# Attention followed by a PReLU MLP: the result parts turned by VectorE in 32x32 blocks and placed by the store, instead of by TensorE and ScalarE

## The chip, the cores and the metric

The kernel runs on one core of a Trainium2 chip. The metric is the device time of one execution in microseconds (us), as the median of several executions. A core has five engines that run side by side and wait for one another by semaphores: PE (TensorE, the matrix unit; its weight loads are shown apart as PEld), DVE (VectorE), ACT (ScalarE), POOL (GpSimd) and SP (SyncE, which here only issues DMA transfers). SBUF is the working memory, with 128 partitions; PSUM is the small memory that PE writes its products to, in eight banks.

## What is computed

The reference, cut to what matters:

```python
# q, k, v: (4, 8, 768, 64); proj: (64, 6)
q_bucket = np.sum((np.einsum('bhsd,dk->bhsk', q, proj) > 0) * 2 ** np.arange(6), axis=-1)
k_bucket = np.sum((np.einsum('bhsd,dk->bhsk', k, proj) > 0) * 2 ** np.arange(6), axis=-1)
mask = q_bucket[:, :, :, None] == k_bucket[:, :, None, :]
scores = np.where(mask, scale * np.matmul(q, k.transpose(0, 1, 3, 2)), -1e9)
attn = np.exp(scores - np.max(scores, axis=-1, keepdims=True))
attn = attn / (np.sum(attn, axis=-1, keepdims=True) + 1e-09)
x = np.matmul(attn, v)                 # then (B,H,S,D) -> (B*S, H*D): 3072 x 512
# w_in: (512, 2048), w_out: (2048, 512), alpha: (2048,)
h = x @ w_in
g = np.maximum(h, 0.0) + alpha * np.minimum(h, 0.0)
out = g @ w_out                        # 3072 x 512, float32
```

An attention in which a query sees only the keys of its own hash bucket, and then two matrix products with a PReLU between them.

## The kernel before

The attention runs first, in 32 units `u` (16 pairs of heads, two halves of the queries each). While it runs, DVE and ACT also prepare the weights of the MLP. Then come 60 blocks of products, for each of the 4 batches 8 blocks `ff1` (names `f` in the profile) and 7 blocks `ff2` (names `z`). The products use a scheme with seven multiplications instead of eight at two levels (a Strassen form), so that each block needs sums of its operands, which DVE makes, and a block of `ff2` has seven steps of eight matmul instructions.

The result of `ff2` is kept transposed: `m2[b, p]` holds output columns in its partitions (`i` is the upper or lower 128 of 256) and tokens in its free dimension. `turn_out` brings it into the order of the output. It runs when a part is complete, four times for each batch, 16 times in all.

```python
    def load_w2(b, n):
        if n < 7:
            t = late[0].tile([P, NI, 2 * H2], F32, name=f"wl{b}_{n}", tag="wl")
            nc.sync.dma_start(t, w_out_s[SIDES[ORDER[n]][0]])
            for m, kh, dh in ((0, 0, 0), (1, 1, 0), (2, 1, 1), (21, 0, 1)):
                w2[b, n, m] = t[:, kh * HK : (kh + 1) * HK, dh * H2 : (dh + 1) * H2]
    # ... cut ...
    def turn_out():
        while to_turn:
            b, p, half, ch = to_turn.pop(0)
            ps = two_banks(f"to{b}_{p}")
            flat = ps.rearrange("p a f -> p (a f)")
            for t in range(CH):                                   # CH = 3
                for i in range(2):
                    do(PE.transpose(flat[:, 2 * t * P + i * P :][:, :P], m2[b, p][:, i, t * P : (t + 1) * P], ident))
            o = late[0].tile([P, CH, 2 * P], F32, name=f"o{b}_{p}", tag="o")
            do(ACT.copy(o.rearrange("p t d -> p (t d)"), flat[:, : CH * 2 * P]))
            nc.sync.dma_start(
                out_v[b, ch * CH : (ch + 1) * CH].rearrange("c p d -> p c d")[:, :, half * 2 * P : (half + 1) * 2 * P], o,
            )
```

`do` keeps the compute instructions of each engine in the order of the program. The tile pools decide by themselves when a buffer is free, and the transfers may be moved. The block loop (cut):

```python
    for j, (b, what, n) in enumerate(blocks):
        # ... step 2 and its finish, sums for the next block ...
        if j:
            now.step(5); now.step(6); now.step(3)
            turn_out()
            sum_w2(b, n2, 6)
            now.step(7)
            sum_w2(b, n2, 5); sum_g2(b, n2, 5)
        # ... loads of later weights; in the last ff2 block of a batch the four sum_x ...
        before = now
        if j + 1 < len(blocks):
            now = ...                       # the next product
            now.step(1)
        before.step(4)
        # ...
    turn_out()
```

The parts of the attention that the change touches:

```python
    def setup():
        # ...
        ps = psum.tile([P, 512], F32, name="nil", tag="av")
        for i in range(12):                                       # matmuls on zeros while the first loads are under way
            do(PE.matmul(ps, zero[:, :P], zero, start=True, stop=True))

    def setup_alpha():
        ps = psum.tile([P, NF], F32, name="alps", tag="sm")
        # ...
    # in the loop over the units:
        attend(u, 0)          # probabilities times values, key blocks 0, 1, 2 -> tile av
        totals(u)             # ones times the summed probabilities accd -> tile sm
        # ... weight work of DVE ...
        attend(u, 1)          # key blocks 3, 4, 5
        divide(u)
```

Of the kernel before, what the change touches and what calls it, by code (L numbers as in the profile page):

```python
# [8 lines left out]
F32 = mybir.dt.float32  # L9
# [338 lines left out]
@with_exitstack  # L348
def kernel(
    ctx: ExitStack,  # L350
    tc: tile.TileContext,
    q: bass.AP,
    k: bass.AP,
    v: bass.AP,
    proj: bass.AP,
    moe_w_in: bass.AP,
    moe_w_out: bass.AP,
    moe_alpha: bass.AP,
    out: bass.AP,
):  # L360

    args = (tc, q, k, v, proj, moe_w_in, moe_w_out, moe_alpha, out)
    keep = ctx.enter_context(tc.tile_pool(name="keep", bufs=1))
    flag = keep.tile([1, 1], mybir.dt.int32, name="flag")
    fast_path(*args, flag)
    again = tc.nc.values_load(flag[0:1, 0:1])
    with tc.If(again > 0):  # L400
        general_path(*args)
# [3 lines left out]
def fast_path(  # L405
# [12 lines left out]
    nc = tc.nc  # L418
# [78 lines left out]
    def setup():  # L497

        zero = const.tile([P, 512], BF16, name="zero")
        do(DVE.memset(zero, 0.0))  # L500
        do(DVE.memset(wh, 0.0))
        for s in range(2):
            nc.sync.dma_start(wh[D * s : D * s + D, :NB], proj)
        nc.sync.dma_start(alpha16, moe_alpha.rearrange("(t p) -> t p", p=P))
        make_identity(nc, ident)
        do(DVE.memset(ones, 1.0))

        ps = psum.tile([P, 512], F32, name="nil", tag="av")
        for i in range(12):
            do(PE.matmul(ps, zero[:, :P], zero, start=True, stop=True))  # L510

        do(DVE.memset(hb, 0.0))
        for r in range(0, P, 32):
            do(DVE.memset(hb[r : r + 2 * NB], 1.0 if r % D else -1.0))
            do(DVE.memset(hb[r : r + NB], -1e-37))
        for t in pts:
            do(POOL.memset(t[:, :, CW : CW + 1], 1.0))
        for t in qbs:
            do(POOL.memset(t, 0.0))

    def setup_alpha():
        ps = psum.tile([P, NF], F32, name="alps", tag="sm")
        do(PE.transpose(ps, alpha16, ident[:NF, :NF]))
        do(DVE.tensor_copy(alpha, ps))

# [111 lines left out]

    BOTH = slice(0, 2)

    def turn(pi, name, halves=BOTH):  # L640

        src = nat[name, pi].rearrange("p c h d -> p c (h d)")
        if halves.start == 0:
            tr[name, pi] = pool.tile([P, S], F32, name=f"{name}T{pi}", tag=f"{name}T")
        ps = two_banks(f"tp_{name}{pi}")
        for c in range(CH * halves.start, CH * halves.stop):
            do(PE.transpose(ps[:, c // CH, c % CH * P :][:, :P], src[:, c], ident))
        do(ACT.activation(
            tr[name, pi].rearrange("p (h w) -> p h w", h=2)[:, halves], ps[:, halves, :CW], AF.Copy,
            scale=DOWN if name == "q" else 1.0,  # L650
        ))

    def magnitude(pi, name):

# [66 lines left out]
        do(DVE.tensor_tensor(accd[u], accd[u], accp[u], op=ALU.add))  # L721


    def attend(u, half):
        pi, g = divmod(u, NCH)
        if half == 0:
            av[u] = psum.tile([P, 512], F32, name=f"av{u}", tag="av")
        w = CW + 1 if g == 0 else CW
        for kc in range(half * NC // 2, (half + 1) * NC // 2):
            for s in range(2):  # L730
                do(PE.matmul(  # L731
                    av[u][D * s : D * s + D, :w], nat["v", pi][:, s, kc * D : (kc + 1) * D], prob[u, kc][:, s, :w],
                    start=(kc == 0), stop=(kc == NC - 1),
                ))
        if half == 1 and g == 0:
            vsum[pi] = pool.tile([P, 1], F32, name=f"vs{pi}", tag="vs")
            do(DVE.tensor_scalar(vsum[pi], av[u][:, CW : CW + 1], EPS, None, op0=ALU.mult))

# [135 lines left out]
    def load_w2(b, n):  # L874

        if n < 7:
            t = late[0].tile([P, NI, 2 * H2], F32, name=f"wl{b}_{n}", tag="wl")
            nc.sync.dma_start(t, w_out_s[SIDES[ORDER[n]][0]])
            for m, kh, dh in ((0, 0, 0), (1, 1, 0), (2, 1, 1), (21, 0, 1)):
                w2[b, n, m] = t[:, kh * HK : (kh + 1) * HK, dh * H2 : (dh + 1) * H2]  # L880

    def sides_g(b, n):
        t = g_m[b, SIDES[ORDER[n]][1]]
# [54 lines left out]
    def turn_out():  # L938
        while to_turn:
            b, p, half, ch = to_turn.pop(0)  # L940
            ps = two_banks(f"to{b}_{p}")
            flat = ps.rearrange("p a f -> p (a f)")
            for t in range(CH):
                for i in range(2):
                    do(PE.transpose(flat[:, 2 * t * P + i * P :][:, :P], m2[b, p][:, i, t * P : (t + 1) * P], ident))
            o = late[0].tile([P, CH, 2 * P], F32, name=f"o{b}_{p}", tag="o")
            do(ACT.copy(o.rearrange("p t d -> p (t d)"), flat[:, : CH * 2 * P]))
            nc.sync.dma_start(
                out_v[b, ch * CH : (ch + 1) * CH].rearrange("c p d -> p c d")[:, :, half * 2 * P : (half + 1) * 2 * P], o,
            )  # L950


    top = const.tile([P, 4], F32, name="top")
# [29 lines left out]
    setup()  # L983
    load_part(0, "q", slice(CH, NC), nc.sync)
    load_part(0, "k", slice(CH, NC), nc.scalar)
    for name in "qk":
        turn(0, name, first)
    hash_bits(0, first)
    for name in "qk":
        turn(0, name, second)  # L990
    load(1, "q")
    load(1, "k")
    load_weight(0)
# [16 lines left out]
    for u in range(UNITS):  # L1010
        pi, g = divmod(u, NCH)
        scores(u, 1)
        if u < last:
            scores(u + 1, 0)
        add_last(u)
        add_total(u)
        if u < last:
            add_first(u + 1)
        else:
            now = ff1(0, 0)  # L1020
            now.step(1)
            now.step(5)
        if g == 0 and pi + 1 < NPAIR:
            hash_bits(pi + 1)
        if g == 1 and pi + 2 < NPAIR:
            turn(pi + 2, "q")
            turn(pi + 2, "k")
        if u < last:
            weight_parts(u + 1)
        else:  # L1030
            weight_sums(4)
        attend(u, 0)
        totals(u)
        if u < last:
            weight_sum(u + 1)
            weight_sums(1 if u < HW - 1 else 2)
            weight_group(u + 1)
        attend(u, 1)
        divide(u)
        if g == 1 and pi + 2 < NPAIR:  # L1040
            load(pi + 2, "v")
        load_weight(u + 4)
        if u == HW + 2:
            load_w(0)
            load_w(1)
            load_x(0)
        if HW + 4 <= u < HW + 8:
            sum_x(0, u - HW - 4, DVE)
        if u + 2 < NW:
            weight_abs(u + 2)  # L1050
        if u == 1:
            setup_alpha()
        if g == 1:
            for name in "qk":
                magnitude(pi, name)
                if pi + 3 < NPAIR:
                    load(pi + 3, name)
# [8 lines left out]
    for j, (b, what, n) in enumerate(blocks):  # L1066
        n2 = n + 1 if what == "2" else 0 if n == NI - 1 else 7
        if n2 == 0:
            sides_g(b, 0)
            sum_w2(b, 0, 3, 4)  # L1070
        now.step(2) if j else now.step(6)
        if j == 0:
            now.step(3)
            now.step(7)
            now.step(2)
        now.step(22)
        if j == 4:
            largest()
        if 0 < n2 < 7:
            sides_g(b, n2)  # L1080
            sum_w2(b, n2, 3, 4)
        if n2 < 7:
            sum_g2(b, n2, 3, 4)
        if j:
            now.step(5)
            now.step(6)
            now.step(3)
            turn_out()
            sum_w2(b, n2, 6)
            now.step(7)  # L1090
            sum_w2(b, n2, 5)
            sum_g2(b, n2, 5)
        if j == 4:
            verdict()
        if what == "1":
            load_w(b * NI + n + 2)
            if n >= NI - 2:
                load_w2(b, n - NI + 2)
        else:
            load_w2(b, n + 2)  # L1100
            if b + 1 < B:
                if n == 0:
                    load_x(b + 1)
                if n == 6:
                    for m in range(4):
                        sum_x(b + 1, m, DVE)
        before = now
        if j + 1 < len(blocks):
            b1, what1, n1 = blocks[j + 1]
            now = ff1(b1, n1) if what1 == "1" else ff2(b1, n1)  # L1110
            now.step(1)
        before.step(4)
        if n2 < 7:
            sum_g2(b, n2, 6)
    turn_out()
# [1 line left out]
_INS = ['q', 'k', 'v', 'proj', 'moe_w_in', 'moe_w_out', 'moe_alpha']  # L1117
_OUTS = [((3072, 512), 'float32')]
# [25 lines left out]
```

## Time and profile before

| | before |
|---|---|
| time, median of 3 | 924.33 us (924.19 to 925.03) |
| span of the profiled execution | 923.9 us |
| PE busy | 907.8 us (98%) |
| DVE busy | 754.0 us (82%) |
| ACT busy | 422.6 us (46%) |
| attention | from the start to about 363 us |
| one batch of the MLP | about 139 us: 73 us of `f` blocks and 66 us of `z` blocks |

The page of the profile gives the busy time of each engine and, for groups of like instructions, their number, their mean duration and the idle time ahead of them, with what ended that idle time. A line such as "L945 PE MATMUL to<-ident,m 128*128 128x128 f32 x96" is one group: source line 945, engine PE, a matrix instruction that writes tile `to` from `ident` and `m`, and there were 96 of them. For a matmul the first name after the arrow is the operand that streams through, the second the one that is loaded as weights. In a timeline, "[2.87 <-DMA wl]" after a row says that the engine stood idle for 2.87 us until a transfer to `wl` landed. PE's instructions overlap, so the distance from start to start of consecutive ones is their cost, not their duration.

### The profile page before, as it was taken

To read this page: it belongs to the slowest core of one execution; us is meant where nothing else is said; L and a number is where in the kernel's file an instruction comes from. 1 tells how busy PE (TensorE), PEld (TensorE's weight loads), DVE (VectorE), ACT (ScalarE), POOL (GpSimd) and SP (SyncE) were. 2 spreads that over 40 slices of the span, in tenths; PEclk is the share of its full clock that TensorE was granted. 3 is DMA by queue.
4 is the path that set the end of the run, shared out by engine and by line. 5 is a ranking of instruction groups with operands and counts; after the bars stand their busy time and mean duration, and the time that the engine had idled before them with its cause. 6 is when DMAs were issued, how large, how long until landed. Compare 5 with 4: busy or idle time off the path is not lost.

```text
span 923.9 us, 13627 instructions
## 1 busy us (share of the span) xinstructions
PE 907.8 (98%) x5073; PEld 605.4 (66%) x5073; DVE 754.0 (82%) x1316; ACT 422.6 (46%) x751; POOL 40.9 (4%) x50
## 2 busy tenths in 40 slices
PE   7999999999999999999999999999999999999996
PEld 4444444454444444556998556998556998556996
DVE  3899998999999998678987668978668978668985
ACT  7788888888877783222212222212222212222212
POOL 1111111111111110000000000000000000000000
PEclk9999999999999999999999999999999999999999
DMA  9576969798777844425333325334325333321232
GB/s 240 145 188 158 273 162 301 177 254 240 189 188 190 205 131 148 174 92 186 110 134 131 116 101 180 109 131 140 112 105 177 111 133 138 112 105 40 100 131 70
DMA packets 114059, 141.50 MB, mean 153 GB/s; under 512 B 54064, under 2 KB 102208, under 8 KB 110400
## 3 DMA queue, kind: packets, MB, share of 16 engines
q1 hardware_dynamic: 103680, 127.56, 43.4%
q0 software_dynamic: 8704, 12.58, 8.0%
q8 instruction: 42, 0.69, 0.3%
q10 hardware_dynamic: 1600, 0.39, 0.2%
q14 instruction: 33, 0.27, 0.1%
HBM read 100.67 MB, written 27.26 MB: 138 GB/s over the span
## 4 chain that ended last, share of the span: by engine, by line
PE 65%; DVE 16%; DMA 2%; issue 1%; ACT 0%; DVEq 0%; ACTq 0%
PE sc L698 3%; PE z_4a L805 2%; PE f_4a L805 2%; PE z_7a L805 2%; PE z_5a L805 2%; PE z_3a L805 2%; PE z_6a L805 2%; PE z_2a L805 2%; PE z_1a L805 2%; PE f_2a L805 2%; PE f_5a L805 2%; PE f_7a L805 2%; PE f_6a L805 2%; PE f_1a L805 2%; PE av L731 2%; PE f_0a L805 2%
## 5 line engine op out<-in xcount | busy, mean ns | idle before, releaser
L703 ACT ACTIVATE pt<-sc 128x768 f32<-128x768 f32 x192 | 153.1, 814 | 61.8 <-PE sc L698 60.1
L698 PE MATMUL sc<-qT,kT 64*128 64x384 f32 x768 | 155.1, 482 | 0.0
L731 PE MATMUL av<-pt,vn 128*64 128x385 f32 (+1 forms) x768 | 136.5, 491 | 0.0
L731 PEld LDWEIGHTS av<-pt,vn 128*64 128x64 f32 x768 | 52.3, 136 | 70.7 <-issue 63.8
L698 PEld LDWEIGHTS sc<-qT,kT 64*128 64x128 f32 x768 | 68.1, 188 | 34.8 <-issue 34.7
L855 DVE TENSOR_TENSOR g<-g,g 128x384 f32<-128x384 f32 x128 | 68.4, 555 | 2.2
L698 PE MATMUL sc<-qb,kb 64*128 64x384 bf16 x384 | 63.0, 324 | 2.8 <-ACT kb L684 2.2
L895 DVE TENSOR_TENSOR ws<-wl 128x512 f32<-128x512 f32 x56 | 38.5, 688 | 24.0 <-DMA wl<-w_out_s 24.0
L903 DVE TENSOR_TENSOR gs<-g,gs 128x768 f32<-128x768 f32 x56 | 53.5, 956 | 1.0
L903 DVE TENSOR_TENSOR gs<-g 128x768 f32<-128x768 f32 x56 | 53.4, 953 | 0.0
L713 POOL DMA_DIRECT2D accp<-pt x32 | 38.5, 1204 | 311.4 <-DVE accp L712 150.2
L851 DVE SCALAR_TENSOR_TENSOR g<-h,alpha 128x384 f32<-128x384 f32 x32 | 19.8, 618 | 36.0 <-ACT h L844 36.0
L698 PEld LDWEIGHTS <-kb 64*128 64x128 bf16 x384 | 19.2, 94 | 43.2 <-issue 19.9
L712 DVE TENSOR_TENSOR accp<-pt,pt 128x768 f32<-128x768 f32 x32 | 30.4, 951 | 10.0 <-ACT pt L703 10.0
L679 ACT ACTIVATE qb<-hs,hb 32x384 bf16<-32x384 f32 x64 | 36.7, 574 | 2.2 <-issue 1.1
L721 DVE TENSOR_TENSOR accd<-accd,accp 128x768 f32<-128x768 f32 x32 | 30.7, 958 | 5.1 <-DMA accp<-pt 4.1
L717 DVE TENSOR_TENSOR accd<-pt,pt 128x768 f32<-128x768 f32 x32 | 30.5, 952 | 3.6 <-ACT pt L703 3.6
L718 DVE TENSOR_TENSOR accd<-accd,pt 128x768 f32<-128x768 f32 x32 | 30.7, 959 | 3.3
L915 DVE TENSOR_TENSOR m<-m,m 128x768 f32<-128x768 f32 (+1 forms) x40 | 28.6, 716 | 1.9 <-ACT m L921 1.2
L743 PE MATMUL sm<-accd,ones 128*64 128x384 f32 x128 | 26.5, 492 | 3.2 <-DVE accd L721 3.1
L684 ACT ACTIVATE kb<-hs,hb 64x384 bf16<-64x384 f32 (+1 forms) x48 | 27.7, 578 | 0.6
L564 DVE TENSOR_SCALAR_CACHE_REDUCE wx<-wx 128x512 f32<-128x512 f32 x32 | 21.7, 679 | 2.9 <-ACT wx L558 2.9
(323 smaller groups left out, 1777.7 us busy)
## 6 DMA issues: line engine op xcount, KB each, us to landing
wi<-w_in_s SPq DMA_DIRECT2D x32, 896.0 KB, 4.6
wl<-w_out_s SPq DMA_DIRECT2D x28, 1024.0 KB, 4.8
accp<-pt POOLq DMA_DIRECT2D x32, 384.0 KB, 4.3
raw<-in_moe_w_in_dram SPq DMA_DIRECT2D x16, 512.0 KB, 4.0
raw<-in_moe_w_out_dram SPq DMA_DIRECT2D x16, 512.0 KB, 3.8
w_in_s<-wsi SPq DMA_DIRECT2D x16, 448.0 KB, 5.4
w_out_s<-wso SPq DMA_DIRECT2D x8, 896.0 KB, 5.5
vn<-in_v_dram SPq DMA_DIRECT2D x16, 384.0 KB, 4.5
```

The lines of the kernel that those rows point to most:

```text
L679: do(ACT.activation(bits["q", pi][D * s : D * s + 32, cols], ps[c : c + 32, half, :CW], AF.Sign, bias=hb[c : c + 32],))
L698: do(PE.matmul(sc[:, s, :CW], what["k", pi][r, ks], what["q", pi][r, qs], start=first, stop=not first,))
L703: do(ACT.activation(pt[:, :, :CW], sc[:, :, :CW], AF.Exp, scale=SCALE / DOWN))
L713: nc.gpsimd.dma_start(accp[u], p(u, 2), accum_op=ALU.add)
L717: do(DVE.tensor_tensor(accd[u], p(u, 3), p(u, 4), op=ALU.add))
L718: do(DVE.tensor_tensor(accd[u], accd[u], p(u, 5), op=ALU.add))
L721: do(DVE.tensor_tensor(accd[u], accd[u], accp[u], op=ALU.add))
L731: do(PE.matmul(av[u][D * s : D * s + D, :w], nat["v", pi][:, s, kc * D : (kc + 1) * D], prob[u, kc][:, s, :w], start=(kc == 0), stop=(kc = ...
L805: do(PE.matmul(self.ps[bank], self.left(left, k), self.right(right, k), start=start and k == 0, stop=k == self.nk - 1, skip_group_check=no ...
L855: do(DVE.tensor_tensor(new_g(b, to)[:, i], g_m[b, x][:, i], g_m[b, y][:, i], op=ALU.subtract))
L895: do(DVE.tensor_tensor(t, w2[b, n, x], w2[b, n, y], op=op))
L903: do(DVE.tensor_tensor(t, g2[b, n, x], g2[b, n, y], op=ALU.subtract))
```

## The change

The main part: an `m2` part is no longer turned by PE (six 128x128 transposes into PSUM) and moved by ACT (a copy of 128x768). DVE turns it in 32x32 blocks, with two instructions of 128x384, one for each `i`, straight from SBUF to SBUF. A turn in 32x32 blocks puts each block right inside, but leaves the blocks of the four partition groups where they are. The store then puts the blocks in place: twelve transfers of 32 partitions x 4 x 64 elements, instead of one of 128 x 3 x 256. So that a row piece in memory is 64 elements long (256 bytes) and not 32, the two halves `i` are not the upper and lower 128 columns any more but the even and odd ones: DVE writes half `i` to every second element of `o`, and the weights of `ff2` are read as every second column of the loaded tile. `turn_out` moves to the end of the block, behind the sums. The very last part is still turned by PE and ACT, in two pieces with a store each.

Small parts: at the start 8 instead of 12 matmuls on zeros, and DVE instead of ACT copies the turned `k` of pair 0; `alpha` is turned in another PSUM buffer; and in each unit of the attention `totals` comes after five of the six key blocks instead of three.

The diff, cut to its core:

```diff
-        for i in range(12):
+        for i in range(8):
             do(PE.matmul(ps, zero[:, :P], zero, start=True, stop=True))
 ...
-        ps = psum.tile([P, NF], F32, name="alps", tag="sm")
+        ps = two_banks("alps")[:, 0, :NF]
 ...
+        if engine is DVE:
+            do(DVE.tensor_copy(dst, ps[:, halves, :CW]))
+        else:
+            do(ACT.activation(dst, ps[:, halves, :CW], AF.Copy, scale=DOWN if name == "q" else 1.0))
 ...
-                w2[b, n, m] = t[:, kh * HK : (kh + 1) * HK, dh * H2 : (dh + 1) * H2]
+                w2[b, n, m] = t.rearrange("p n (f i) -> p n i f", i=2)[:, kh * HK : (kh + 1) * HK, dh]
 ...
     def turn_out():
         while to_turn:
             b, p, half, ch = to_turn.pop(0)
-            ps = two_banks(f"to{b}_{p}")
-            ... six PE.transpose, o, ACT.copy, one dma_start ...
+            o = late[0].tile([P, CW, 2], F32, name=f"o{b}_{p}", tag="o")
+            for i in range(2):
+                do(DVE.transpose(o[:, :, i], m2[b, p][:, i]))
+            src = o.rearrange("p (c w d) i -> p c w (d i)", c=CH, d=32)
+            for a in range(DM // 128):
+                for c in range(CH):
+                    cols = slice(half * DM // 2 + 64 * a, half * DM // 2 + 64 * a + 64)
+                    nc.sync.dma_start(
+                        out_v[b, ch * CH + c].rearrange("(w r) d -> r w d", r=32)[:, :, cols],
+                        src[32 * a : 32 * a + 32, c],
+                    )
+
+    def turn_last():
+        ((b, p, half, ch),) = to_turn
+        ps = two_banks("to").rearrange("p a f -> p (a f)").rearrange("p (t i f) -> p t i f", i=2, f=P)
+        o = late[0].tile([P, CH, P, 2], F32, name="o_last", tag="o")
+        for ts in ((2,), (0, 1)):
+            for i in range(2):
+                for t in ts:
+                    do(PE.transpose(ps[:, t, i], m2[b, p][:, i, t * P : (t + 1) * P], ident))
+            ts = slice(ts[0], ts[-1] + 1)
+            do(ACT.copy(o[:, ts].rearrange("p t f i -> p t i f"), ps[:, ts]))
+            ... one dma_start of o[:, ts] ...
 ...
-    for name in "qk":
-        turn(0, name, first)
-    hash_bits(0, first)
-    for name in "qk":
-        turn(0, name, second)
+    for half in (first, second):
+        turn(0, "q", half)
+        turn(0, "k", half, DVE)
+        if half is first:
+            hash_bits(0, first)
 ...
-        attend(u, 0)
+        attend(u, range(NC - 1))
         totals(u)
 ...
-        attend(u, 1)
+        attend(u, range(NC - 1, NC))
         divide(u)
 ...
             now.step(3)
-            turn_out()
             sum_w2(b, n2, 6)
 ...
+        turn_out()
         before = now
 ...
-    turn_out()
+    turn_last()
```

More of the change, by code (lines that the diff above doesn't have):

```diff
@@ L638, in fast_path, with turn @@
     BOTH = slice(0, 2)
-    def turn(pi, name, halves=BOTH):
+    def turn(pi, name, halves=BOTH, engine=None):
         src = nat[name, pi].rearrange("p c h d -> p c (h d)")
@@ L647, in turn @@
             do(PE.transpose(ps[:, c // CH, c % CH * P :][:, :P], src[:, c], ident))
[L648 to L651, printed above, removed]
+        dst = tr[name, pi].rearrange("p (h w) -> p h w", h=2)[:, halves]
+        if engine is DVE:
+            do(DVE.tensor_copy(dst, ps[:, halves, :CW]))
+        else:
+            do(ACT.activation(dst, ps[:, halves, :CW], AF.Copy, scale=DOWN if name == "q" else 1.0))
     def magnitude(pi, name):
@@ L721, in add_total, with attend @@
         do(DVE.tensor_tensor(accd[u], accd[u], accp[u], op=ALU.add))
-    def attend(u, half):
+    def attend(u, kcs):
         pi, g = divmod(u, NCH)
-        if half == 0:
+        if kcs.start == 0:
             av[u] = psum.tile([P, 512], F32, name=f"av{u}", tag="av")
         w = CW + 1 if g == 0 else CW
-        for kc in range(half * NC // 2, (half + 1) * NC // 2):
+        for kc in kcs:
             for s in range(2):
@@ L734, in attend @@
                 ))
-        if half == 1 and g == 0:
+        if kcs.stop == NC and g == 0:
             vsum[pi] = pool.tile([P, 1], F32, name=f"vs{pi}", tag="vs")
@@ L940, in turn_out @@
             b, p, half, ch = to_turn.pop(0)
-            ps = two_banks(f"to{b}_{p}")
[L942 to L950, printed above, removed]
+            o = late[0].tile([P, CW, 2], F32, name=f"o{b}_{p}", tag="o")
[19 more added lines that the diff above has]
+            do(ACT.copy(o[:, ts].rearrange("p t f i -> p t i f"), ps[:, ts]))
+            dst = out_v[b, ch * CH : (ch + 1) * CH].rearrange("c p d -> p c d")
+            nc.sync.dma_start(dst[:, ts, half * 2 * P : (half + 1) * 2 * P], o[:, ts].rearrange("p t f i -> p t (f i)"))
     top = const.tile([P, 4], F32, name="top")
```

## The prediction

> **What bounds the kernel now.** I began with the page: engines, slices, chain.
>
> ```profile
> PE 907.8 (98%) x5073; PEld 605.4 (66%) x5073; DVE 754.0 (82%) x1316; ACT 422.6 (46%) x751; POOL 40.9 (4%) x50
> ...
> DVE  3899998999999998678987668978668978668985
> ...
> PE 65%; DVE 16%; DMA 2%; issue 1%; ACT 0%; DVEq 0%; ACTq 0%
> ```
>
> PE is busy for 98% of the span and carries most of the chain that ended last, so what leaves PE shortens the run, unless another engine then makes PE wait. DVE comes next: it holds 16% of the chain, and the chain listed by stretches has it from about 154 to 277 us, in the attention. In the MLP (from the 16th slice on) the chain lies on PE. Busy time by stretches, for the `z` and `f` blocks of the first batch (columns: length, PE, PEld, DVE, ACT, POOL, clock, DMA share, GB/s):
>
> ```profile
> 432.24:497.94 65.70, 65.70 (x408) 65.04 (x406) 57.32 (x91) 13.90 (x38) 0.00 (x0) 1.00 0.39 135
> 497.94:571.20 73.26, 73.12 (x235) 43.63 (x235) 50.27 (x89) 19.64 (x41) 0.00 (x0) 1.00 0.36 123
> ```
>
> PE never rests in the `z` stage, and DVE is at 57.32 / 65.70 = 87%. The timeline around one `turn_out` (start, length):
>
> ```profile
> 456.97 1.46 PE L805 MATMUL z_5c<-g,ws 128*128 128x192 f32 x8
> ...
> 458.27 0.82 PE L945 MATMUL to<-ident,m 128*128 128x128 f32 x6
> ...
> 458.92 1.47 PE L805 MATMUL z_5a<-gs,ws 128*128 128x192 f32 x8
> 459.12 0.80 ACT L947 COPY o<-to 128x768 f32<-128x768 f32 x1 [1.58 <-PE to L945]
> 459.95 0.39 SPq L948 DMA_DIRECT2D out_dram<-o  x1
> ```
>
> A step of eight matmuls takes 458.27 - 456.97 = 1.30 us, 162.5 ns each, and the six transposes push the next step back by 458.92 - 458.27 = 0.65 us, 108 ns each. ACT's copy stands on nobody's path. Last, what PE waited for over the run:
>
> ```profile
> PE sm L743 <- DVE accd L721: 3.1, 6, 0.8
> PE sc L698 <- ACT kb L684: 2.2, 2, 1.2
> PE nil L510 <- DVE wh L501: 1.2, 1, 1.2
> PE alps L523 <- DVE st L753: 1.0, 1, 1.0
> PE to L945 <- DVE m L915: 0.7, 1, 0.7
> ```
>
> These few microseconds are what the small parts can win.
>
> **What the Trainium skill says.** "VectorE: DVE Perf Modes", The three transpose paths: DVE turns 32x32 blocks only, so the transfers have to place them. The trace agrees on what such an instruction costs: the attention's own turns of 128x384 took 574 and 578 ns. "SBUF — State Buffer", Door 1 (its note on cachelines): SBUF is read in lines of 16 bytes and a stride is free while at least two elements fall into each line, thus every second fp32. No instruction of the trace before reads weights that way, so the run has to show it. "TensorE: Matmul & The Clock Gate", LDWEIGHTS: a load takes the number of columns / 1.2, 107 ns for 128. The trace agrees: a transpose with its own weight load passes every 108 ns. "DMA: Bandwidth & Descriptors", Specifications: transfers under 512 B per piece are not at line rate. The trace agrees loosely: the `q` loads in 256-byte pieces land in 4.3 us (192 KB, 768 pieces), the stores of `x` of the same size in longer rows in 3.5 us.
>
> **The change, part by part.**
>
> *Removed from PE and ACT.* Of 16 parts, 15 leave PE: 15 x 0.65 = 9.75 us. The fifteenth lies in the last block, where it belongs to the tail, so 14 x 0.65 = 9.1 us come out of the stream of full steps. ACT loses 15 x 0.80 us, off the path.
>
> *Added to DVE.* 30 instructions; by the attention's turns 0.58 us each, 1.15 us for a part. Two parts fall into a batch's `z` stage, the third about its end, the fourth into the first `f` block. The `z` stage goes to 57.3 + 2.3 = 59.6 us of DVE in 65.7 - 1.95 = 63.75: 93%. Is it in time? DVE's timeline has idle stretches of 0.25, 1.48, 2.87, 0.88 and 0.25 us in the second to sixth `z` block, all while `wl` is landing. Part 2 comes in the third block (1.48 idle, of which 0.65 go because the block gets shorter), part 3 in the sixth (0.25). Part 3 leaves DVE about 1.5 us late. In that block the sum `gs_4_3` is ready at 488.28 and its step begins at 492.25: 4.0 us of slack. The tightest buffer, the PSUM bank `c`, is read by DVE until 489.5 and written again at 492.25. So no wait of PE comes from this.
>
> *Strided weights.* Steps 1, 2 and 4 of seven read `wl` directly: 672 of the 1568 `z` matmuls. A load needs at most 108 ns (the transposes) and has 162.5 ns: it could grow by half before it shows. I count 0.
>
> *The stores.* 12 transfers instead of one. An issue takes 0.32 us for the 128-piece stores of `x` and 0.39 us for the stores of `o`; 12 x 0.33 = 4.0 us of SP for each part. By the order of the built program the loads of `wl` and `wi` keep their places: part 2's stores come behind `wl_4`, part 3's behind `wl_0` of the next batch, part 4's behind the first free `wi`. The next load comes a block (9.1 us) later, and SP is free again. In 1536 pieces of 256 B a store takes more time in the DMA engines than before, but their share is 0.39 and 0.36 here. I count 0 until the tail.
>
> *The tail.* In the last block PE saves the 0.65 us of part 5. I replay the end with the times of before: step 7 at 912.22 instead of 912.87, step 4 at 914.15, the last sums of DVE till 916.47, and the two turns of part 5 just before (914.9 to 916.0). The last piece is turned by four transposes and a copy of 2/3 of the size, ready at about 917.6 instead of 918.77. But SP issues in order, and part 5's twelve stores stand first: 916.05 + 4.0 = 920.0, then the two last ones; the last issue is at about 920.4, where it was at 918.80. The tail gets 1.6 us longer. MLP in sum: -9.1 + 1.6 = -7.5.
>
> *The start.* The matmuls on zeros begin at 1.19 us; their weight loads stand about 0.42 us apart up to the eighth, at about 4.1, and the last four fit into 0.75 us. Turning begins at 5.18 us. With eight it could begin at about 4.35, when the first `q` (issue at 0.74 to 1.7, 2.4 to 2.5 us to landing) is there. The chain on ACT and PE up to the first exponential then moves by 0.8 us: -0.8. DVE's copy of `k` shortens only what is already parallel for the first half, and frees 0.49 us of ACT before the first exponential, which waits for PE: 0.
>
> *`totals` later.* Four more matmul pairs (8 x 0.162 = 1.3 us) stand ahead of it. The waits are 0.8 us at most in the row above; by starts, `av` to `sm` is 1.99 us undisturbed (45.62 to 47.61) and 2.91 at the worst (347.09 to 350.00), so 0.92. Each is covered. Where DVE is the limit the gain is one time 1.3 us for each stretch in which PE has caught up with it: 0.7 at the first unit, 1.3 at 261 to 300, 1.0 in the last two units: -3.0. `divide` still has the next unit's scores (4.95 us) to finish under.
>
> *`alpha`.* PE's wait of 1.0 us goes, but a score buffer is held until DVE has its copy: -0.3.
>
> Sum: 924.3 - 7.5 - 0.8 - 3.0 - 0.3 = 912.7; I take 913.
>
> **Rivals.** *The strided weight loads become the limit.* For it: PEld is busy for 65.04 of 65.70 us in the `z` stage, and such a read is untried here. Against it: these 190 ns loads overlap, and the transposes pass in 108 ns. If a strided load took double (216 ns), 672 x 53 ns = 36 us would come on top: about 949. *DVE becomes the bound of the `z` stage.* For it: 93%, and turns that write every second element, or sums that read so, may be slower than the 0.58 and 0.69 us used. If each turn took 1.0 us, two parts would ask for 1.7 us more of each `z` stage's 4.1 spare; only with the 13 sums on `wl` also slower would PE wait, by some microseconds for each batch: 915 to 925. *The stores delay the loads.* The part 2 stores are in the engines with `wl_4`; `wl` landed at 468.05 and step 1 of its block began at 469.16, so 1.1 us late is enough. For it: 1536 small pieces. Against it: the load is issued first. If every store cost a wait of 1 us: 15 us, and nothing is gained. *The tail hides.* If the issue of a small store is faster (0.2 us), the tail costs nothing: 911.
>
> **Range and chances.** The core is well founded: 9.1 us of PE time counted from starts. The small parts (-4.1) could come to half or to a little more, the tail to between 0 and 3, late loads or DVE to several. Eight in ten: 908 to 920. Faster by over 2% would need under 905.8 and has no source in this sum: 0.03. Slower by over 2% (over 942.8) is only the strided weights: 0.06. Within 2%: 0.91.
>
> **What would show it.** Right: the steps beside a turn stand 1.30 us apart without a gap; steps on `wl` take 1.30 us like those on `ws`; DVE turns of about 0.58 us; no PE wait for `wl`, `wi` or `ws` in the MLP; twelve issues in about 4 us, the last store behind them. Wrong: `wl` steps over 1.30 us, PE waits for DVE `gs` or `ws` in the `z` blocks, a wait for a DMA, or a first turn that still begins at about 5 us.

## The result, and the profile after

| | before | after |
|---|---|---|
| time, median | 924.26 us (923.65 to 925.1) | 921.38 us (920.55 to 923.39) |
| ratio to before, 95% interval | 1 | 0.997 (0.9957 to 0.9983) |
| span of the profiled execution | 923.9 us | 920.6 us |

The change brings 2.9 us, where 11 were predicted. The page of the changed kernel, engines and chain:

```profile
PE 896.8 (97%) x4979; PEld 596.7 (65%) x4979; DVE 768.4 (83%) x1348; ACT 409.5 (44%) x735; POOL 40.9 (4%) x50
...
PE 76%; DVE 16%; DMA 4%; issue 1%; SPq 1%; ACT 1%; DVEq 0%; ACTq 0%; POOLq 0%
```

PE lost 11.0 us of work and DVE took over 14.4, as meant. But the span fell by less than a third of what PE lost, and the chain that ended last now has SyncE's queue in it (SPq 1%), which it had not before. Busy time by stretches, again for the `z` and the `f` blocks of the first batch:

```profile
431.88:495.62 63.74, 63.74 (x390) 63.15 (x389) 58.38 (x94) 11.47 (x35) 0.00 (x0) 1.00 0.42 135
495.62:567.87 72.25, 72.25 (x230) 43.11 (x230) 52.77 (x95) 18.80 (x40) 0.00 (x0) 1.00 0.41 129
```

The `z` stage is 63.74 us long (65.70 before) and PE never rests in it; DVE is at 58.38, or 92%. The timeline around a turn (start, length):

```profile
461.82 1.46 PE L808 MATMUL z_6b<-g,wl 128*128 128x192 f32 x8
...
463.12 1.46 PE L808 MATMUL z_6c<-gs,ws 128*128 128x192 f32 x8
...
464.42 1.46 PE L808 MATMUL z_6a<-gs,ws 128*128 128x192 f32 x8
...
464.78 1.03 DVE L946 STREAM_TRANSPOSE o<-m 128x384 f32<-128x384 f32 x2
465.72 1.46 PE L808 MATMUL z_6c<-g,ws 128*128 128x192 f32 x8
...
465.84 4.14 SPq L952 DMA_DIRECT2D out_dram<-o  x9
```

The steps stand 1.30 us apart, past the turn and no matter whether the weights are summed ones (`ws`) or every second column of the loaded tile (`wl`). Nine small stores take SP 4.14 us. So the middle of the kernel does what was wanted. The end does not. SP's queue in the last 21 us (start, length of a row of issues), first before, then after, with two narrower cuts:

```profile
918.80 0.37 SPq L948 DMA_DIRECT2D out_dram<-o  x1
```

```profile
900.60 12.65 SPq L952 DMA_DIRECT2D out_dram<-o  x24
913.35 1.74 SPq L969 DMA_DIRECT2D out_dram<-o_last  x2
...
906.55 6.70 SPq L952 DMA_DIRECT2D out_dram<-o  x12
...
914.70 0.40 SPq L969 DMA_DIRECT2D out_dram<-o_last  x1
```

Part 3's twelve stores are just out when part 5's twelve begin at 906.55, and the two of the last part, whose first piece ACT copied at 907.54, stand behind them till 914.70. PE is done at about 908.6. What PE waited for:

```profile
PE av L734 <- DVE x L762: 2.3, 4, 0.9
PE sc L701 <- ACT kb L687: 2.2, 2, 1.1
PE sc L701 <- DVE alpha L526: 1.7, 1, 1.7
PE to L965 <- ACT o_last L967: 1.3, 1, 1.3
PE nil L512 <- DVE wh L503: 1.2, 1, 1.2
PE f_2a L808 <- DMA wi<-w_in_s: 1.1, 2, 0.7
```

The 3.1 us for `sm` and the 1.0 for `alps` are gone from the top. In their place stand a wait of the values product `av` for DVE's division (2.3), one of the attention products `sc` for `alpha`'s copy (1.7), and one of the third `f` product for its input weights (1.1).

**The theory, and its rival.** To compare runs I cut each profiled span at three starts of PE: of the step `f_1b` in the first batch, of the first `f_2a`, and of the last `z_4b`. The table has the length of each stretch in us; the kernels below the second row are the experiments told in the next section.

| kernel | to `f_1b` | to `f_2a` | to the last `z_4b` | to the end | span |
|---|---|---|---|---|---|
| before | 371.17 | 6.45 | 529.40 | 16.8 | 923.9 |
| after | 369.85 | 7.31 | 520.55 | 22.9 | 920.6 |
| main part only | 370.61 | 6.45 | 520.01 | 23.7 | 920.7 |
| small parts only | 369.88 | 6.87 | 529.25 | 16.8 | 922.8 |
| late parts 3 and 5 on PE | 368.75 | 6.74 | 520.52 | 17.2 | 913.3 |
| stores on two queues | 368.68 | 7.05 | 520.64 | 20.4 | 916.7 |
| `alpha` back | 369.15 | 6.80 | 519.96 | 23.4 | 919.3 |
| totals back | 370.45 | 6.45 | 519.91 | 23.4 | 920.2 |
| input weights first | 371.78 | 6.45 | 519.94 | 23.8 | 922.0 |
| late part 5 on PE | 369.43 | 6.80 | 520.28 | 17.0 | 913.6 |
| the best: late part 5 on PE, own buffer, input weights first | 370.42 | 6.45 | 519.74 | 16.7 | 913.3 |
| late parts 3 and 5 on PE, own buffer, input weights first | 370.71 | 6.45 | 520.76 | 17.2 | 915.1 |
| late parts 3 and 5 on PE, own buffer | 371.94 | 6.92 | 520.75 | 16.8 | 916.4 |

Theory A: the stream gains its 9 us, the small stores at the end take 6 of them back, and the small parts bring next to nothing. Rival B: the small parts brought their 4 us, and DVE's turns cost it somewhere. The first column scatters: kernels whose compute is in the same order up to `f_1b` stand between 368.68 and 371.94. So the small parts are judged by the waits for `sm` and `av`, which repeat, and by the times.

### The profile page after: what moved, and what is told of

It reads as the page before. It is cut to its first block, busy times and chain, and to the rows that moved or that the text cites. A ratio compares the mean times of both kernels' runs of the same rounds, so it can differ in the third digit from the quotient of the medians.

```text
span 920.6 us, 13660 instructions
## 1 busy us (share of the span) xinstructions
PE 896.8 (97%) x4979; PEld 596.7 (65%) x4979; DVE 768.4 (83%) x1348; ACT 409.5 (44%) x735; POOL 40.9 (4%) x50
## 4 chain that ended last, share of the span: by engine, by line
PE 76%; DVE 16%; DMA 4%; issue 1%; SPq 1%; ACT 1%; DVEq 0%; ACTq 0%; POOLq 0%
PE sc L701 11%; PE av L734 9%; PE f_2a L808 2%; PE z_6a L808 2%; PE z_5a L808 2%; PE z_2a L808 2%; PE z_1a L808 2%; PE f_5a L808 2%; PE f_7a L808 2%; PE f_6a L808 2%; PE f_4a L808 2%; PE f_3a L808 2%; PE z_3a L808 2%; PE f_0a L808 2%; PE f_1a L808 2%; PE sm L746 1%
## 5 line engine op out<-in xcount | busy, mean ns | idle before, releaser
L808 PE MATMUL f_2a<-x,wi 128*128 128x384 f32 x64 | 23.5, 489 | 1.1 <-DMA wi<-w_in_s 1.1
```

The source lines that it names most:

```text
L808: do(PE.matmul(self.ps[bank], self.left(left, k), self.right(right, k), start=start and k == 0, stop=k == self.nk - 1, skip_group_check=no ...
```

## The experiments

**1. The main part alone.** The changed kernel with the four small parts undone.

```diff
-        for i in range(8):
+        for i in range(12):
-        ps = two_banks("alps")[:, 0, :NF]
+        ps = psum.tile([P, NF], F32, name="alps", tag="sm")
-        turn(0, "k", half, DVE)
+        turn(0, "k", half)
-        attend(u, range(NC - 1))
+        attend(u, range(NC // 2))
-        attend(u, range(NC - 1, NC))
+        attend(u, range(NC // 2, NC))
```

> The change with its small parts undone: twelve nil products at the start, both halves of k copied by ScalarE, alpha in its own small buffer, the totals after three key blocks. What is left of the change is the result parts turned by VectorE and the strided weights. The marker is the start of the first product f_0a (363.32 us in the kernel before, 362.01 in the changed one). Theory A (the three small parts are worth little by the end, because the wait for input weights at the second product of the first MLP absorbs them; the new tail alone eats the gain of the stream): total about 921.7 us, 2.6 less than before; f_0a back at about 363.3; no wait for input weights at f_2a beyond 0.1 us; the four output stages still 2.6 us shorter each; tail from the last z_4b to the end 22.9 us. Rival B (the small parts gave their 4.1 us as predicted and the VectorE turns cost it elsewhere): total about 925 us, slower than before.

Measured: 921.89 us, ratio to before 0.9971 (0.9958 to 0.9983), the same as the whole change. The stream is within 0.6 us and the tail within 0.8 us of the changed kernel's, and `f_2a` does not wait. The marker `f_0a` came at 362.77, half a microsecond off, inside the scatter.

**2. The small parts alone.** The kernel before with the four edits above turned round, so that the result parts are still turned by PE and stored in one piece.

```diff
-        for i in range(12):
+        for i in range(8):
-        ps = psum.tile([P, NF], F32, name="alps", tag="sm")
+        ps = two_banks("alps")[:, 0, :NF]
 ...
+        turn(0, "k", half, DVE)
 ...
-        attend(u, 0)
+        attend(u, range(NC - 1))
 ...
-        attend(u, 1)
+        attend(u, range(NC - 1, NC))
```

> The kernel before with only the small parts of the change: eight nil products, k copied by VectorE, alpha in a half of the score buffer, the totals after five key blocks. The result parts are still turned by TensorE and stored in one piece. Theory A: f_0a starts about 1.3 us earlier (near 362.0), and f_2a then waits about 0.7 us for its input weights, so that the total is 923.5 to 923.9 us, 0.4 to 0.8 less than before. Rival B (the small parts are worth 4.1 us): total about 920 us.

Measured: 924.12 us, ratio 1.0003 (0.9992 to 1.0015): between 0.7 us less and 1.4 us more than before. The 4.1 us that I had counted for them lie far outside. Rival B falls with these two runs. The wait of `f_2a` was 0.3 us and not 0.7.

**3. Both late parts turned by PE.** Parts 3 and 5 of the last batch go the old way: six transposes, a copy, one store each. The other parts keep DVE's turns.

```diff
+            if b == B - 1 and p in (3, 5):
+                ps = ...                                   # as before: two PSUM banks
+                ... six PE.transpose of m2[b, p] ...
+                o = late[0].tile([P, CH, P, 2], F32, name=f"o{b}_{p}", tag="o")
+                do(ACT.copy(o.rearrange("p t f i -> p t i f"), ps))
+                ... one dma_start of o ...
+                continue
```

> The changed kernel, except that the two late parts 3 and 5 of the last batch are turned by TensorE and copied by ScalarE as before, with one store each in the place of twelve small ones. The other 22 parts keep the VectorE turns. Theory A (the tail is 6.0 us longer because SyncE issues 24 small stores one after the other at 0.53 us each, ahead of the last two): TensorE works 2 x 0.65 = 1.3 us more, the last store is issued at about 911 instead of 915.1 us, and the total falls to about 915.5 us, 5.9 less than the changed kernel. Rival B (only the 1.3 us that the last copy waits for an output buffer matter, the stores' issue does not): total about 919.5 us, 2 less.

(Of the 15 parts that DVE turns in the changed kernel 13 keep its turns; the 22 of the expectation is a slip.) Measured: 915.29 us, ratio 0.9911 (0.9892 to 0.993), 6.1 us less than the changed kernel. SP's queue at the end:

```profile
904.26 0.39 SPq L951 DMA_DIRECT2D out_dram<-o  x1
905.43 1.73 SPq L981 DMA_DIRECT2D out_dram<-o_last  x2
```

The last two stores go out as soon as their copies are done, although PE works longer. Two microseconds (rival B) would not do. It does not yet say what about the stores costs the time: their issue, or the pieces themselves.

**4. Six of the stores on another queue.** The pieces stay as they are; six of part 5's twelve are issued by ACT, after its copies.

```diff
+                    if b == B - 1 and p == 5 and (a + c) % 2:
+                        held.append(store)
+                    else:
+                        nc.sync.dma_start(*store)
 ...
     turn_last()
+    for store in held:
+        do(nc.scalar.dma_start(*store))
```

> The changed kernel, except that six of the twelve small stores of part 5 of the last batch are issued from ScalarE's queue, after its last copies; 18 of the 24 late small stores stay with SyncE. All the pieces are the same and as small. Theory A (what ends the kernel is the issue of small stores one after the other on SyncE): six issues of 0.53 us leave the chain, less what ScalarE adds after its copies at 909.3 us (six issues, to about 912.5): total about 918.2 to 918.9 us, 2.4 to 3.2 less than the changed kernel. Rival B (the DMA engines are the limit, which need their time for the 512-byte pieces whoever issues them): no change, about 921.4 us.

(The pieces are of 256 bytes; the 512 of the expectation is a slip.) Measured: 918.1 us, ratio 0.9935 (0.9917 to 0.9953), 3.3 us less than the changed kernel. The tail alone, without the scatter of the attention, is 2.5 us shorter (20.4 against 22.9 in the table). SP's rows at the end, and ACT's:

```profile
899.15 8.84 SPq L961 DMA_DIRECT2D out_dram<-o  x18
908.10 0.88 SPq L975 DMA_DIRECT2D out_dram<-o_last  x2
...
907.25 4.24 ACTq L1142 DMA_DIRECT2D out_dram<-o  x6
```

The DMA engines (the last two columns: their busy share, and GB/s) while part 5's stores are issued, first in the changed kernel, then here:

```profile
906.55:913.35 6.80, 0.74 (x5) 0.42 (x4) 0.36 (x1) 1.21 (x3) 0.00 (x0) 0.74 0.35 63
905.20:911.50 6.30, 0.74 (x5) 0.42 (x4) 0.36 (x1) 1.21 (x3) 0.00 (x0) 0.77 0.55 126
```

The same bytes in the same pieces leave. SP is done at 908.98, where it was 915.09, and ACT's six issues, the last done at 911.49, now come last. Meanwhile the DMA engines move 126 GB/s, twice what they moved in the changed kernel, and are busy for 55% and not 35%. They had room, so their work on the pieces was not the limit; the issue one after the other on one queue was. It fits what the Trainium skill says ("Perfetto Trace Analysis", DMA Instruction — HWDGE (DVE, Sync)): the profiled length of such an issue ends where the sequencer is free for its next instruction. In the trace of the changed kernel the next small store begins 0.045 us behind it. On ACT the six issues took between 0.32 and 1.25 us each; their row of 4.24 us also holds 0.68 us between the second and the third, in which ACT waited.

**5. `alpha` back in its small buffer.**

```diff
-        ps = two_banks("alps")[:, 0, :NF]
+        ps = psum.tile([P, NF], F32, name="alps", tag="sm")
```

> The changed kernel, with alpha's broadcast in its own small buffer again, where the totals also go. The prediction put the move of alpha at -0.3 us. Theory A (once the totals come later, either place costs one wait of TensorE on VectorE at the same point, 1.7 us for the score buffer when VectorE runs late, 0.2 when it doesn't, about 1.7 for the small buffer, which VectorE reads until 39.3 us while TensorE stands ready at 37.5): the broadcast itself waits 1.4 to 1.9 us and the scores behind it don't wait for alpha; total within 1 us of the changed kernel. Rival B (the move brings its 0.3 us or more, its wait was 1.0 us and vanished): the broadcast waits about 1.0 us and the total is 0.3 to 1 us longer, not to be told by the total alone.

Measured: 921.38 us (ratio 0.9966, 0.9951 to 0.9981), and no wait of PE for the broadcast at all, which neither theory had. In this run DVE stood 1.4 us earlier at that point: it read `sm` from 37.29 on, where the changed kernel has it at 38.67. So the size stays open. Over the traces with `alpha` in the score buffer PE's wait for its copy was 1.7 us in four, 2.1, 1.4 and 0.3 in one each, and in three too short to be listed; with the small buffer it was 1.0 before, and nothing in the two experiments that have it. In the six with 1.4 us or more, DVE begins its turn of `sm`, which stands ahead of its copy of `alpha`, 0.8 to 1.5 us after PE's broadcast; in the four others it begins 0.3 to 0.5 us before it. So the wait depends on how late DVE is against PE, and the move shows no gain.

**6. The totals back after three key blocks.** The last two edits of experiment 1 alone.

> The changed kernel, with the totals of the exponentials taken after three key blocks again in the place of five. The prediction put the later totals at -3.0 us, from the 2.7 to 3.1 us that TensorE waits for VectorE's sums. Theory A (the later totals only exchange this wait for one for the buffer of the weighted values, which the division leaves later): TensorE waits 2.8 to 3.1 us (six times) ahead of the totals again, the 2.3 us (four times) ahead of the weighted values go to nothing, the sum changes by 0.4 to 0.7 us, total within 1 us of the changed kernel. Rival B (the later totals bring 3.0 us): total about 924 us.

Measured: 922.46 us, ratio 0.9979 (0.9971 to 0.9987), whose interval meets that of the changed kernel. PE's waits:

```profile
PE sm L746 <- DVE accd L724: 3.2, 6, 0.8
PE sc L701 <- ACT kb L687: 2.2, 2, 1.1
```

The 3.2 us for the sums are back and the 2.3 for `av` are gone. So the later totals exchange one wait for another: 3.2 against 0.3 + 2.3, a gain of 0.6 us, not 3.0.

**7. The input weights first.** The first two loads of the output weights (1 MB each) of the first batch come behind the input weights of the third product.

```diff
-            if n >= NI - 2:
-                load_w2(b, n - NI + 2)
+            if n in (1, 2) if b == 0 else n >= NI - 2:
+                load_w2(b, n - 1 if b == 0 else n - NI + 2)
```

(Cut: these three loads also keep their place in the order of the program.)

> The changed kernel, with the first two loads of the output weights (1 MB each) put behind the load of the input weights of the third product in the first batch, so that these no longer queue behind 2 MB. Theory A (what the attention gained by its end, up to 1.3 us, is taken again by TensorE's wait for these input weights, 0 to 1.1 us from run to run): this wait at f_2a vanishes; total 0.4 to 1.0 us less than the changed kernel, about 920.6. Rival B (the loads' order costs nothing by the end of the kernel): total as the changed kernel, and the output stage may wait for its first weights instead.

Measured: 921.54 us, ratio 0.9965 (0.995 to 0.9979). The wait at `f_2a` is gone (6.45 us from `f_1b`, as before the change, in the table), but its share is smaller than the times can show.

**8. Only part 5 by PE.** As experiment 3, with `p == 5`.

> The changed kernel, except that part 5 alone of the last batch is turned by TensorE and copied by ScalarE, with one store; part 3 keeps the VectorE turn and its twelve small stores. Against the kernel in which both were turned by TensorE TensorE works 0.65 us less. Theory A (twelve small stores from about 898.5 us take SyncE 12 x 0.5 = 6 us, to 904.5, which still lies ahead of the last stores at about 904.8): total about 914.7 us, 0.6 less than with both parts on TensorE (915.3). Rival B (the twelve still stand before the last stores, or the last copy waits for part 3's buffer): 915.5 to 917 us.

Measured: 914.95 us, ratio 0.9891 (0.9874 to 0.9907). It can't be told from experiment 3 by its time, but the trace says which stores mattered:

```profile
899.23 5.56 SPq L964 DMA_DIRECT2D out_dram<-o  x12
904.89 0.40 SPq L951 DMA_DIRECT2D out_dram<-o  x1
906.59 1.74 SPq L981 DMA_DIRECT2D out_dram<-o_last  x2
```

Part 3's twelve stores are out at 904.79, before anything else wants the queue. So it is part 5's twelve that cost the changed kernel its 6 us. But the second half of rival B came true: ahead of the last part's first copy ACT waited 0.60 us, till 906.18, for the buffer that the small stores held.

**9. Three versions with a buffer of their own for the last part.** Part 5 by PE and the input weights first; parts 3 and 5 by PE and the input weights first; parts 3 and 5 by PE alone.

```diff
-        o = late[0].tile([P, CH, P, 2], F32, name="o_last", tag="o")
+        o = late[0].tile([P, CH, P, 2], F32, name="o_last", tag="o_last", bufs=1)
```

> The version with part 5 of the last batch turned by TensorE and part 3 by VectorE, with two additions: the last part's output tile gets a buffer of its own, and the first two loads of the output weights of the first batch come behind the input weights of the third product. Theory A (the last copy's wait of 1.2 us, 0.6 of it beyond the transposes before it, is for the buffer that part 3's small stores hold, and falls on the end): the wait goes, total about 914.0 us, 0.9 less than without the additions (914.95). Rival B (the last stores cannot start sooner, because SyncE still has part 5's store before them): about 914.9 us.

> Parts 3 and 5 of the last batch turned by TensorE, the last part's output tile in a buffer of its own, and the first loads of the output weights behind the input weights. Theory A: with both parts on TensorE the buffer was no wait beyond 0.5 us; total about 914.9 us, 0.4 less than without the additions (915.29). Rival B (TensorE's 0.65 us for part 3 lie under something else, and all else is equal): as the version with part 5 alone, about 914.0 us.

> Parts 3 and 5 of the last batch turned by TensorE and the last part's output tile in a buffer of its own, the loads in the changed kernel's order. Against the version with the loads turned round it shows what their order is worth. Theory A (TensorE's wait for the third product's input weights, 0 to 1.1 us from run to run, is paid in full): 0.3 to 0.6 us more than with the order turned round, about 915.2. Rival B (worth nothing): the same, within 0.3 us.

Measured: 913.62 us (0.9885, 0.9868 to 0.9901), 916.11 us (0.9911, 0.9894 to 0.9928) and 916.68 us (0.9912, 0.9891 to 0.9934). In the first the wait is gone: the last part's stores go out at 905.98, 0.85 us after part 5's.

```profile
899.48 5.56 SPq L964 DMA_DIRECT2D out_dram<-o  x12
905.13 0.40 SPq L951 DMA_DIRECT2D out_dram<-o  x1
905.98 1.74 SPq L981 DMA_DIRECT2D out_dram<-o_last  x2
```

It is the best version found, 0.85% under the changed kernel (0.9885 / 0.997). The intervals of experiments 3, 8 and of these three overlap; what the own buffer and the order of the loads bring singly is not resolved. The second and third came out 1.2 and 1.5 us above their expectations, and their tails (17.2 and 16.8 us) don't show it: the profiled runs reached `f_1b` at 370.71 and 371.94, late in the scatter.

## Why the prediction was wrong, point by point

| step of the prediction | predicted, us | measured, us |
|---|---|---|
| 14 parts leave the stream | -9.1 | -8.9 from `f_2a` to the last `z_4b` in the changed kernel, -8.6 to -9.7 over all with DVE's turns |
| strided weights | 0 | 0 (steps at 1.30; a load 5 to 7 ns longer) |
| DVE's turns, in time | 0 | 0 (0.556 each, `z` stage 63.74 of 63.75 predicted, DVE 92% of 93%) |
| stores against the loads | 0 | 0.4 (one wait for `wi` at 786.2) |
| the tail | +1.6 | +6.0 |
| start, totals, `alpha` | -4.1 | between -0.7 and +1.4 (experiment 2) |

**The middle was right**: the stream gave 8.9 of 9.1 us. The Trainium skill's "SBUF — State Buffer" (Door 1, cachelines) let me expect that weights at every second fp32 load at full speed. Nearly so: the 672 strided loads took 194 to 197 ns each in the trace, the packed ones 190 before and after. The steps take the same 1.30 us: with a matmul every 162.5 ns, loads of 190 or 197 ns must overlap with the matmuls, and the longer ones do not show. How much longer a load could get before it shows was not tried.

One point of it is not quite nothing. The chain that ended last, in the changed kernel, has this stretch (start, length):

```profile
776.04 1.89 SPq L952
780.88 5.28 DMA wi<-w_in_s
786.20 1.56 PE f_2a L808 x4
```

Small stores of the third batch, one of which held SP for 1.89 us, lie ahead of an input load there, and PE waited 0.39 us for it. This is the rival "the stores delay the loads", with 0.4 us where it had 15.

**The tail was mis-sized.** The prediction had seen that "part 5's twelve stores stand first", and its replay of DVE held: the stores were to begin 9.03 us after the start of the last `z_4b` (916.05 - 907.02) and began after 8.84 (906.55 - 897.71). The step that failed is "12 x 0.33 = 4.0", and with it the 0.4 us that were left for the first store of the last part. I had taken the length of one issue from stores with as many pieces. A small one takes 0.43 us in the median, with 0.045 to the next, so twelve take 5.56 us where nothing disturbs them (part 3's row), 1.6 more than counted. In part 5's row three were longer still (0.56, 1.19 and 0.71 us), and it took 6.70 us. The first store of the last part took 1.25 instead of 0.4. The last issue thus stood 16.99 us behind the start of `z_4b` (914.70 - 897.71), 3.6 later than predicted (920.4 - 907.02 = 13.4). From the last issue to the end it took 5.9 us where it was 5.1, another 0.8 that the prediction did not have. That is not the store's own time: the last one landed 2.2 us after its issue, against 3.0 before. What came after the landing took longer, and why was not looked into. So 1.6 + 3.6 + 0.8 = 6.0. Experiment 3 takes the issues of parts 3 and 5 away and gets 5.6 us of the tail back, experiment 8 those of part 5 alone and gets 5.8; experiment 4 moves half of part 5's to another queue and gets 2.5.

The four longer issues make up 2.0 of the 3.6 us (6.70 - 5.56 and 1.25 - 0.40), and the number of stores does not explain them. The page of the changed kernel lists two DMA queues of the kind `instruction`, which by this name bring in the program (packets, MB, share of the engines):

```profile
q8 instruction: 41, 0.67, 0.3%
q14 instruction: 36, 0.29, 0.1%
```

In the trace each of the four has a packet of one of these queues beside it, of 8 or 16 KB, that took 0.31 to 1.07 us; beside the 1.89 us issue at 776.04 there is one of 1.49 us. Over the eleven kernels with small stores, 43 issues of result stores took more than 0.55 us. Each of the 43 has such a packet (over 0.25 us) under way or ended less than 1 us before; of the 1871 shorter ones 301 have. No run moved these packets, so it is likely, and not shown, that they are what holds up the issues.

**`totals` later** fell on the sentence that "`divide` still has the next unit's scores (4.95 us) to finish under". The `av` tile has one buffer: DVE's division frees it, and the division now starts two key blocks later. The next unit's `av` waits for it, 0.3 to 0.9 us, four times. The wait was moved, as experiment 6 shows, with 0.6 us left of 3.0. **`alpha`** was the same mistake, small: a buffer of the attention products is held until DVE comes round, and costs PE up to 2.1 us where the old wait was up to 1.0.

**The start** gave 0.3 us between the traces before and after (first attention product at 9.18 instead of 9.47), not 0.8; the small parts alone have it at 9.09, the main part alone at 10.55. From run to run this point moves between 8.52 and 10.44 with the same compute in the same order, so its size stays open.

**What the attention still gained was partly taken at the next hand-over.** The input weights of `f_2a` queue behind 2 MB of output weights that are requested when the attention ends: 0.86 us more between `f_1b` and `f_2a` in the changed kernel, 0 to 0.6 in the others. I had named late loads as a risk of the stores, not of the attention's gain. That this is worth half a microsecond is what the waits say; the times can't show it.

The range, 908 to 920, missed the result by 1.4 us: the tail was allowed "between 0 and 3" and was 6, and the small parts were to come "to half or to a little more", and came to about none.

## What to carry to other kernels

Replacing one store by many small ones is free only where the issuing queue has time before the next thing that it must send; count issues in series by their own measured length, and keep the last parts of a kernel on the path with the fewest issues, even if that gives work back to the busiest engine. Before a wait is scheduled away, ask which single-buffered tile will now be freed later, because the wait tends to come back there. And an optimisation need not be applied everywhere: 14 of 16 parts gave all the gain, and one of the other two took two thirds of it back.

## What the runs showed of the hardware that was not expected

- An issue of a 32-partition store in 256-byte pieces held SP for 0.43 us in the median (0.32 to 1.89), plus 0.045 to the next; a store of `x`, which also has 128 pieces, held it for 0.33 us in the median. All 43 of over 0.55 us, in eleven kernels, have a packet of a queue of the kind `instruction` beside them.
- DVE's 32x32 turn of 128x384 fp32 from SBUF took 556 ns in the mean while writing every second element, no more than the attention's turns into closely packed tiles (574 and 578 ns). These read PSUM, or one element many times over; a packed turn from SBUF was not run, so the price of the stride alone is not shown.
- A weight load of every second fp32 took 194 to 197 ns where a packed one takes 190, and the steps of eight matmuls stayed at 1.30 us.
- The same order of compute reaches the same point of the MLP with a scatter of 3.3 us between profiled runs, 368.68 to 371.94 us. Its cause was not looked for. A gain of a microsecond in the attention is therefore shown by waits and by several times, not by a single pair of traces.
